# A planned attention-and-FFN kernel: transposes issued in groups, the planner's matmul price by stream and next load, plain heads on 128 rows, weights converted in pieces of 512 columns

## The chip, the core and the metric

The kernel runs on one core of a Trainium2 chip. The metric is device time in microseconds (us): a median over runs, and beside it one profiled execution, whose trace tells what each engine did. TensorE (PE) multiplies, VectorE (DVE), ScalarE (ACT) and GpSimd (POOL) do the elementwise work, and SyncE (SP) issues the DMAs.

## What is computed

Block-causal attention over 8 batches of 8 heads (576 tokens, 64 dimensions, blocks of 64), then a feed-forward network on all 4608 tokens:

```python
scores = scale * np.matmul(q, k.transpose(0, 1, 3, 2))
mask = block_i >= block_j
scores = np.where(mask, scores, -1000000000.0)
scores = scores - np.max(scores, axis=-1, keepdims=True)
attn = np.exp(scores)
attn = attn / (np.sum(attn, axis=-1, keepdims=True) + 1e-09)
x = np.matmul(attn, v)          # heads side by side: (4608, 512)
h = x @ w_in                    # 512 -> 2048
g = np.maximum(0.01 * h, h)
out = g @ w_out                 # 2048 -> 512
```

q, k and v are 32-bit floats; w_in and w_out arrive as 64-bit floats; the kernel takes their bits apart and makes 32-bit values of them.

## The kernel before

**Precision.** A product that must be exact to 32 bits is made of faster matmuls: each operand is split into a high part and a low remainder (`xh`, `xl`; `wih`, `wil`; `gh`, `gl`; `pth`, `ptl`), and three partial products are summed. Heads called plain use whole 32-bit operands instead; one such matmul is two records in the trace.

**Work.** Each of the 64 heads goes through scores into `p_s`, a mask, row maxima (`nm`), the exponentials with their sums (`prow`, `sums`), reciprocals (`rec`), normalising, transposes of `prow` through PE against the identity into the two banks of `p_t`, and the product with V, which is then copied into `xr`. A head's scores come in two parts: tiles 0 to 3 first (eight matmuls in a full head), then tile 4 (four matmuls of 288 columns), which uses the same PSUM and so waits for the exponentials of the first part. The eight heads of the first batch are done in two halves: "lo" (tokens 0 to 319) and "hi" (320 to 575), all with plain products, and with plain scores but for one "hi" head. Heads 8 to 63 are "full" and split.

**FFN.** Tokens go through the FFN in 18 chunks of 256. `split_x` makes `xh` and `xl`; then for each of eight units `u`, `ffn1` does two blocks of twelve matmuls into `p_h` (line 734), followed by the activation into `g`, its split into `gh` and `gl`, and `ffn2` does two blocks of six into `p_o` (line 753). A chunk can start when the heads of its tokens are done, so the first starts after the eight "lo" heads, the second after the "hi" heads, and the third only after eight full heads.

**Weights.** `weight_piece` loads 256 KB into one of six `raw` buffers, makes a 32-bit value in one of six `val` buffers by an ACT copy and two or three integer operations on DVE (lines 397, 401, 406; the sign of every third piece is done by ACT and POOL instead), and splits it. There are 64 pieces. Their converting runs beside the first sixteen heads. Full heads start when it is over, since some of their tiles take the space of the conversion.

**Order.** Nothing is issued in the order of the code. `Plan` collects every operation with its rank, costs and dependences, and a list scheduler at build time (`Plan.run`) walks through modelled time and, for each free engine, takes the ready operation of lowest rank. The constants RL to AHEAD set ranks relative to the head's number. Where PE has nothing ready early on, a `fill` matmul of the identity is inserted. The result is a fixed instruction order on each engine. In this order, transposes (kind "short") are woven one by one between the matmuls of an `ffn2` block (kind "long"):

```python
while a or b:
    if b:
        mixed.append(b.pop(0))
    if a:
        mixed.append(a.pop(0))
```

Of the kernel before, what the change touches and what calls it, by code (L numbers as in the profile page):

```python
# [17 lines left out]
P = 128  # L18
BLK = 64
D = 64  # L20
# [3 lines left out]
EPS = 1e-9  # L24
CH = 256

HS = 7
SIGNS = 3

WIDE = 256  # L30
RAWS = 6
VALS = 6

RL = 7.153
RP = 0.885
RB = 0.516
RT = 1.485
RV = 1.932
RX = -0.113
RN = -0.908  # L40

LEAD = 1.751
LAG = 1.627
RS = 0.514
RG = -0.26
OFF1 = 4.574
SL1 = 11.938
AHEAD = -0.663

LAT = 1550  # L50
HOLD = 567.499

PATIENCE = 424.599
FILL = 235
FILLTO = 12

# [1 line left out]
LOAD = 108  # L58
RATE = 0.4414
# [1 line left out]


class Plan:

# [34 lines left out]
    def run(self):  # L102
# [10 lines left out]
        free = dict.fromkeys(ready, 0)  # L113
        port = {"DVE": 0, "POOL": 0}
        order, now, moved, done = [], 0, 0, 0
        load, start, stream = -LOAD, 0, 0

        def offer(i):
            for k, choice in enumerate(self.ops[i][0]):
# [11 lines left out]
                if not left[j]:  # L131
                    offer(j)

        def multiply(matmuls):
            nonlocal load, start, stream
            for cost, fn in matmuls:
                if now < SLOW:
                    cost *= 2
                load = max(load + LOAD, start, now - 57)
                start = max(start + stream, load + 57, now)  # L140
                stream = cost
                order.append(fn)
            return start + stream

        def best(kind):
            found = [x for x in ready["PE"] if self.ops[x[1]][4] == kind and not ends[x[1]]]
            return min(found) if found else None

        for i in range(total):
            if not left[i]:  # L150
# [1 line left out]
        while done < total:  # L152
# [6 lines left out]
            for e, q in ready.items():  # L159
# [5 lines left out]
                if other:  # L165
                    open_ = port[other] <= now
                    can = [x for x in q if not ends[x[1]] and (open_ or (e == "DVE" and self.ops[x[1]][0][x[2]][0] == "DVE"))]
                    if not can:
                        wake.append(port[other])
                        continue  # L170
                    x = min(can)
                    q.remove(x)
                    heapq.heapify(q)
                elif e == "PE":
                    live = [x for x in q if not ends[x[1]]]
                    x = min(live)
                    short, long_ = best("short"), best("long")
                    if self.ops[x[1]][4] == "short" and not long_:
                        other_ = [y for y in live if self.ops[y[1]][4] != "short"]
                        if other_ and now < since[x[1]] + PATIENCE:  # L180
                            x = min(other_)
                    kind = self.ops[x[1]][4]
                    if kind == "long":
                        self.fill = None
                    if kind in ("short", "long") and short and long_:
                        a = [(c, f, short[1]) for c, f in self.ops[short[1]][0][0][1]]
                        b = [(c, f, long_[1]) for c, f in self.ops[long_[1]][0][0][1]]
                        mixed = []
                        while a or b:
                            if b:  # L190
                                mixed.append(b.pop(0))
                            if a:
                                mixed.append(a.pop(0))
                        at = {}
                        for c, f, i in mixed:
                            at[i] = multiply([(c, f)])
                        free[e] = start + stream
                        for y in (short, long_):
                            q.remove(y)
                            end(y[1], e, at[y[1]])  # L200
                        heapq.heapify(q)
                        continue
                    q.remove(x)
                    heapq.heapify(q)
                    free[e] = multiply(self.ops[x[1]][0][x[2]][1])
                    end(x[1], e, free[e])
                    continue
                else:
                    x = heapq.heappop(q)
# [48 lines left out]
def attention_ffn(ctx: ExitStack, tc: tile.TileContext, qk: bass.AP, v: bass.AP, w_in: bass.AP, w_out: bass.AP, out: bass.AP):  # L258
# [162 lines left out]
    def attention(i):  # L421
# [5 lines left out]

        qkt, qkey = qk_in[z], ("qkt", z)
        plain_s, plain_v = kind == "lo" or kind == "hi" and h < HS, kind != "full"
        rows = D if plain_s else P  # L430
        odd = kind == "lo" and z == 1
        sk = "h" if odd else "s"

# [3 lines left out]
        def row(t, n, c, w):  # L437
            at, c0 = {0: (3, 256), 1: (3, 0), 2: (4, 0)}[t] if odd else (t, 0)
            return prow[y][at][:n, c0 + c : c0 + c + w]
# [21 lines left out]
        rp = r0 - RP  # L461
        q_in, k_in = qkt[:rows, 0, qa:qe], qkt[:rows, 1, :ke]
        if plain_s:
            add(copying(qe - qa, lambda: q_in, lambda: q_in, by=scale), rp, [], [qkey])
            qkd = [qkey]
        else:
            qd, khd, kld = qs[z][:, qa:qe], kh[z][:, :ke], kl[z][:, :ke]
# [100 lines left out]
        for base, c0, w, items in tgroups[kind]:  # L568
            x = bank()

            def transpose(t, j, c, x=x):
                n = P if kind == "full" else qn[t]
                return RATE * n, lambda: nc.tensor.transpose(p_t[x][:, c : c + n], row(t, n, j * P, P), ident[:n, :n])  # L573

            add([("PE", [transpose(*y) for y in items])], r0 + RT, [k for t in sorted({a for a, _, _ in items}) for k in pkeys(t)], [("t", x)], kind="short")
            src = p_t[x][:, c0 : c0 + w]
            if plain_v:
                hi = ptf[:, base : base + w]
# [258 lines left out]
```

## Time and profile before

| | |
|---|---|
| median of 3 runs | 1193.65 us (1190.58 to 1194.34) |
| the profiled execution: its time, its span | 1194.37 us, 1192.3 us |
| busy share of the span | PE 99%, DVE 57%, ACT 55%, POOL 36% |
| chain that ended last | PE 96%, DVE 2%, ACT 1% |
| lines on that chain | p_o L753 33%, p_h L734 33%, p_t L573 9%, p_t L635 8% |
| granted clock, mean | 0.996 |
| read from memory, written | 64.57 MB, 9.44 MB |

The span is the time from the first to the last profiled instruction; the execution's own time is a little longer. A share of busy time is an average over stages, and matmuls overlap each other, so a PE that is always "busy" may still be late: what tells is the distance between the starts of matmuls.

### The profile page before, as it was taken

To read this page: it belongs to the slowest core of one execution; us is meant where nothing else is said; L and a number is where in the kernel's file an instruction comes from. 1 tells how busy PE (TensorE), PEld (TensorE's weight loads), DVE (VectorE), ACT (ScalarE), POOL (GpSimd) and SP (SyncE) were. 2 spreads that over 40 slices of the span, in tenths; PEclk is the share of its full clock that TensorE was granted. 3 is DMA by queue.
4 is the path that set the end of the run, shared out by engine and by line. 5 is a ranking of instruction groups with operands and counts; after the bars stand their busy time and mean duration, and the time that the engine had idled before them with its cause. 6 is when DMAs were issued, how large, how long until landed. Compare 5 with 4: busy or idle time off the path is not lost.

```text
span 1192.3 us, 21079 instructions
## 1 busy us (share of the span) xinstructions
PE 1175.5 (99%) x7778; PEld 1041.4 (87%) x7778; DVE 680.2 (57%) x1782; ACT 657.4 (55%) x1652; POOL 431.5 (36%) x505
## 2 busy tenths in 40 slices
PE   9999899899999999999999999999999999999998
PEld 7877789788899988898999988898998888899997
DVE  5999987766656666644444456665666666310000
ACT  6988866655655565554554455555555555422222
POOL 3233344324443443423332343443444343212222
PEclk9999999899999999999999999999999999999999
DMA  6656422211212111110211211112121210000000
GB/s 175 185 173 193 128 88 72 66 60 55 67 51 70 52 55 60 37 64 30 62 39 35 67 49 55 47 51 69 52 69 46 70 31 30 1 18 1 18 19 18
DMA packets 39592, 75.37 MB, mean 63 GB/s; under 512 B 4032, under 2 KB 23040, under 8 KB 39488
## 3 DMA queue, kind: packets, MB, share of 16 engines
q1 hardware_dynamic: 39488, 74.02, 20.2%
q8 instruction: 61, 1.00, 0.3%
q14 instruction: 43, 0.35, 0.1%
HBM read 64.57 MB, written 9.44 MB: 62 GB/s over the span
## 4 chain that ended last, share of the span: by engine, by line
PE 96%; DVE 2%; ACT 1%; DMA 0%; issue 0%; ACTq 0%; DVEq 0%
PE p_o L753 33%; PE p_h L734 33%; PE p_t L573 9%; PE p_t L635 8%; PE p_s L494 8%; PE p_t L625 2%; PE p_s L488 2%; PE p_o L806 2%; DVE nm L512 1%; PE p_h L488 0%; DVE ptl L284 0%; DVE prow L550 0%; DMA qk_in<-in_qk 0%; ACT prow L521 0%; DMA raw<-in_w_in 0%
## 5 line engine op out<-in xcount | busy, mean ns | idle before, releaser
L285 POOL TENSOR_TENSOR gl<-g,gh 128x512 fp32r<-128x512 f32 x136 | 176.8, 1300 | 460.6 <-ACT gh L274 311.3
L734 PE MATMUL p_h<-xh,wih 128*128 128x256 f32 x1152 | 323.2, 281 | 0.0
L734 PE MATMUL p_h<-xl,wih 128*128 128x256 f32 x1152 | 320.1, 278 | 1.1 <-DVE xl L284 1.1
L734 PE MATMUL p_h<-xh,wil 128*128 128x256 f32 x1152 | 319.9, 278 | 0.0
L521 ACT ACTIVATE prow<-p_s,nm 128x192 f32<-128x192 f32 (+4 forms) x308 | 161.8, 529 | 151.4 <-DVE nm L512 95.4
L573 PE MATMUL p_t<-ident,prow 128*128 128x128 f32 x960 | 239.7, 274 | 3.1 <-DVE ptl L284 0.9
L734 PEld LDWEIGHTS p_h<-xl,wih 128*128 128x128 f32 x1152 | 216.9, 188 | 4.6 <-DVE xl L284 1.3
L734 PEld LDWEIGHTS p_h<-xh,wih 128*128 128x128 f32 x1152 | 216.9, 188 | 4.5 <-issue 1.0
L753 PE MATMUL p_o<-wol,gh 128*128 128x512 f32 x576 | 219.9, 453 | 0.0
L734 PEld LDWEIGHTS p_h<-xh,wil 128*128 128x128 f32 x1152 | 217.0, 188 | 0.0
L741 ACT ACTIVATE g<-p_h 128x512 f32<-128x512 f32 x144 | 85.7, 595 | 234.4 <-PE p_h L734 234.1
L753 PE MATMUL p_o<-woh,gh 128*128 128x512 f32 x576 | 204.0, 426 | 0.0
L753 PE MATMUL p_o<-woh,gl 128*128 128x512 f32 x576 | 192.2, 415 | 0.0
L549 POOL TENSOR_SCALAR prow<-prow,rec 128x192 f32<-128x192 f32 (+4 forms) x214 | 119.1, 568 | 167.1 <-DVE rec L536 124.3
L284 DVE TENSOR_TENSOR ptl<-p_t,pth 128x512 fp32r<-128x512 f32 (+1 forms) x224 | 125.1, 567 | 63.0 <-ACT pth L274 59.6
L614 DVE TENSOR_TENSOR xr<-p_t,xr 64x64 f32<-64x64 f32 x112 | 50.4, 450 | 164.6 <-ACT xr L274 164.3
L573 PEld LDWEIGHTS p_t<-ident,prow 128*128 128x128 f32 x960 | 130.2, 141 | 13.9 <-DVE ptl L284 1.9
L512 DVE TENSOR_REDUCE nm<-p_s 128x1 f32<-128x192 f32 (+4 forms) x308 | 139.7, 486 | 4.6
L753 PEld LDWEIGHTS p_o<-wol,gh 128*128 128x128 f32 x576 | 108.6, 188 | 35.6
L753 PEld LDWEIGHTS p_o<-woh,gh 128*128 128x128 f32 x576 | 105.5, 189 | 28.1 <-issue 2.6
L274 ACT CAST pth<-p_t 128x384 fp32r<-128x384 f32 (+3 forms) x175 | 81.5, 469 | 63.9 <-PE p_t L573 59.5
L753 PEld LDWEIGHTS p_o<-woh,gl 128*128 128x128 f32 x576 | 96.6, 189 | 20.0
(77 smaller groups left out, 1623.9 us busy)
## 6 DMA issues: line engine op xcount, KB each, us to landing
qk_in<-in_qk SPq DMA_DIRECT2D x56, 576.0 KB, 3.7
v_stage<-in_v SPq DMA_DIRECT2D x56, 160.0 KB, 2.2
out<-ob SPq DMA_DIRECT2D x35, 256.0 KB, 2.0
raw<-in_w_in SPq DMA_DIRECT2D x32, 256.0 KB, 3.0
raw<-in_w_out SPq DMA_DIRECT2D x32, 256.0 KB, 3.2
qk_in<-in_qk SPq DMA_DIRECT2D x8, 160.0 KB, 3.0
vf<-in_v SPq DMA_DIRECT2D x8, 160.0 KB, 3.2
vf<-in_v SPq DMA_DIRECT2D x8, 128.0 KB, 2.6
```

The source lines that it names most:

```text
L274: one = lambda: nc.scalar.copy(dst(), src())
L284: ("DVE+" if sb else "DVE", dve(n), lambda: nc.vector.tensor_sub(dst(), one(), two())),
L285: ("POOL", pool2(n), lambda: nc.gpsimd.tensor_sub(dst(), one(), two())),
L494: go = lambda ap=ap, cols=cols, kk=kk, k0=k0, k1=k1, first=first, last=last: nc.tensor.matmul(ap, qs[z][:, cols], kk[:, k0:k1], start=firs ...
L512: [("DVE", dve(kw[t]), lambda t=t, ap=ap, flat=flat: nc.vector.tensor_reduce(nm[z][: qn[t], t : t + 1], ap[: qn[t]], axis=AX.X if flat els ...
L521: nc.scalar.activation(o, ap[: qn[t]], AF.Exp, bias=nm[z][: qn[t], t : t + 1], scale=1.0, accum_out=sums[z][: qn[t], t : t + 1])
L549: ("POOL", pool1(kw[t]), lambda: nc.gpsimd.tensor_scalar(p(), p(), by, 1.0, op0=ALU.mult, op1=ALU.mult)),
L573: return RATE * n, lambda: nc.tensor.transpose(p_t[x][:, c : c + n], row(t, n, j * P, P), ident[:n, :n])
L635: nc.tensor.matmul(to, vs[z][:, j, :], src, start=start, stop=stop)
L734: nc.tensor.matmul(hh[:, i, :], w[:, d, f * P : (f + 1) * P], x[:, d, :], start=k == 0, stop=k == len(terms) - 1)
L741: add([("ACT", act(512), lambda: nc.scalar.activation(g, hh, AF.Prelu, alpha=0.01))], rank, [("h", z)], ["g"])
L753: nc.tensor.matmul(p_o[m], a[:, i, m * P : (m + 1) * P], w[:, 2 * u + i, :], start=u == 0 and k == 0, stop=u == NU - 1 and k == 5,)
```

## The change

It has four parts. The planner no longer weaves transposes into `ffn2` blocks: each group of transposes is one operation, issued in one piece. Its price of a matmul becomes the larger of two things, the stream of the one ahead and a load (108 ns) that begins when the one ahead has started, and not before the operation's inputs are there; a transpose is priced at a stream of 27 ns. All "hi" heads have plain scores (HS 8), and plain heads take 128 rows of q and k, where the array holds q and k twice, with half the scale. Weights are converted in 32 pieces of 512 columns (512 KB) with rings of three, and every fifth piece has its sign done by ACT and POOL. All ranks and the delay for an operation's second choice of engine (HOLD) have new numbers.

```diff
-HS = 7
-SIGNS = 3
-WIDE = 256
-RAWS = 6
-VALS = 6
+HS = 8
+SIGNS = 5
+WIDE = 512
+RAWS = 3
+VALS = 3
...
-RS = 0.514
+RS = 1.479
...
-HOLD = 567.499
-
-PATIENCE = 424.599
+HOLD = 247.855
...
-        def multiply(matmuls):
-            nonlocal load, start, stream
+        def multiply(matmuls, at):
+            nonlocal start, stream
             for cost, fn in matmuls:
                 if now < SLOW:
                     cost *= 2
-                load = max(load + LOAD, start, now - 57)
-                start = max(start + stream, load + 57, now)
+                start = max(start + stream, max(start, at) + LOAD, now)
                 stream = cost
                 order.append(fn)
             return start + stream
...
-                    if kind in ("short", "long") and short and long_:
...
-                    free[e] = multiply(self.ops[x[1]][0][x[2]][1])
+                    x = heapq.heappop(q)
+                    if self.ops[x[1]][4] == "long":
+                        self.fill = None
+                    free[e] = multiply(self.ops[x[1]][0][x[2]][1], since[x[1]])
...
-        rows = D if plain_s else P
+        rows = P
...
-            add(copying(qe - qa, lambda: q_in, lambda: q_in, by=scale), rp, [], [qkey])
+            add(copying(qe - qa, lambda: q_in, lambda: q_in, by=scale / 2), rp, [], [qkey])
...
-                return RATE * n, lambda: nc.tensor.transpose(p_t[x][:, c : c + n], row(t, n, j * P, P), ident[:n, :n])
+                return 27, lambda: nc.tensor.transpose(p_t[x][:, c : c + n], row(t, n, j * P, P), ident[:n, :n])
```

**Around the first p_h.** On PE, from the last part of the "lo" stage to the first FFN matmul, before (`p_o<-ident` is a fill, `p_t<-ident,prow` a transpose, `p_s<-qk_in` a plain score):

```order
L806 MATMUL p_o_110<-ident 128x128 x8
L488 MATMUL p_s<-qk_in_87 128x448
L806 MATMUL p_o_110<-ident 128x128 x17
L573 MATMUL p_t_107<-ident,prow_3_76 128x128
L573 MATMUL p_t_107<-ident,prow_4_77 128x128
...
L806 MATMUL p_o_110<-ident 128x128 x6
L488 MATMUL p_s<-qk_in_87 128x288 x2
L734 MATMUL p_h_108<-xh,wih 128x256
```

and now:

```order
L771 MATMUL p_o_110<-ident 128x128 x8
L453 MATMUL p_s<-qk_in_87 128x448
L771 MATMUL p_o_110<-ident 128x128 x2
L538 MATMUL p_t_107<-ident,prow_3_76 128x128
L538 MATMUL p_t_107<-ident,prow_4_77 128x128
...
L771 MATMUL p_o_110<-ident 128x128 x4
L699 MATMUL p_h_108<-xh,wih 128x256
```

Seventeen fills fewer stand between the last product of a "lo" head and the first p_h, and the two scores of 288 columns have gone behind it. On DVE, the operations ahead of `xl`, which that p_h needs, before:

```order
L284 TENSOR_TENSOR wil<-val_131,wih 128x2x128
L397 TENSOR_SCALAR val_132<-val_132 128x256
L397 TENSOR_SCALAR val_133<-val_133 128x256
L284 TENSOR_TENSOR wol<-val_129,woh 128x256
L401 SCALAR_TENSOR_TENSOR val_132<-raw_126,val_132 128x256
L401 SCALAR_TENSOR_TENSOR val_133<-raw_127,val_133 128x256
L397 TENSOR_SCALAR val_134<-val_134 128x256
L406 SCALAR_TENSOR_TENSOR val_133<-raw_127,val_133 128x256
L401 SCALAR_TENSOR_TENSOR val_134<-raw_128,val_134 128x256
L284 TENSOR_TENSOR xl<-xr_104,xh 128x1024
```

and now:

```order
L500 TENSOR_SCALAR rec_100<-sums_98 128x1
L501 RECIPROCAL rec_100<-rec_100 128x1
L366 SCALAR_TENSOR_TENSOR val_126<-raw_123,val_126 128x512
L515 TENSOR_SCALAR prow_4_77<-prow_4_77,rec_100 128x576
L371 SCALAR_TENSOR_TENSOR val_126<-raw_123,val_126 128x512
L249 TENSOR_TENSOR xl<-xr_104,xh 128x1024
```

`xl` has moved ahead of most of the weight operations; it stands behind two of 512 columns and one normalising.

**Full heads that have one FFN unit each.** On PE before, between the products of the sixth and the seventh full head, from the end of a second score part to the next head's scores:

```order
L494 MATMUL p_s<-kl_93,qs_89 128x288
L573 MATMUL p_t_107<-ident,prow_4_77 128x128
L573 MATMUL p_t_107<-ident,prow_2_75 128x128
...
L573 MATMUL p_t_106<-ident,prow_0_73 128x128
L494 MATMUL p_s<-kh_90,qs_88 128x448
L494 MATMUL p_s<-kh_90,qs_88 128x64
L494 MATMUL p_s<-kl_92,qs_88 128x448
```

and now, between the products of the fifth and the sixth, from the end of a group of eight transposes:

```order
L538 MATMUL p_t_107<-ident,prow_3_1354 128x128
L538 MATMUL p_t_107<-ident,prow_4_1355 128x128
L718 MATMUL p_o_111<-woh,gh_114 128x512 x2
L718 MATMUL p_o_111<-wol,gh_114 128x512 x2
L718 MATMUL p_o_111<-woh,gl_116 128x512 x2
L699 MATMUL p_h_108<-xh,wih 128x256
L699 MATMUL p_h_108<-xl,wih 128x256
L699 MATMUL p_h_108<-xh,wil 128x256
```

Before, nothing of the FFN was left there to put between transposes and scores; now a block of each kind stands in every head of this stage.

**Full heads that have two units each.** On ACT, between the first and the last exponential of a first score part, before:

```order
L521 ACTIVATE prow_3_1612,sums_99<-p_s,nm_97 128x448
L521 ACTIVATE prow_0_1609,sums_99<-p_s,nm_97 64x64
L741 ACTIVATE g<-p_h_108 128x512
L521 ACTIVATE prow_1_1610,sums_99<-p_s,nm_97 128x192
L274 CAST gh_113<-g 128x512
L521 ACTIVATE prow_2_1611,sums_99<-p_s,nm_97 128x320
```

and now:

```order
L486 ACTIVATE prow_3_76,sums_98<-p_s,nm_96 128x448
L486 ACTIVATE prow_0_73,sums_98<-p_s,nm_96 64x64
L239 CAST gh_113<-g 128x512
L486 ACTIVATE prow_1_74,sums_98<-p_s,nm_96 128x192
L486 ACTIVATE prow_2_75,sums_98<-p_s,nm_96 128x320
```

The activation `g` no longer stands among the exponentials.

## Rows read from the trace of the kernel before

**Rows 1.** Windows: per engine busy us (instructions), then granted clock, DMA share, GB/s.

```profile
60.00:140.00 80.00, 78.14 (x454) 60.80 (x454) 73.00 (x213) 67.92 (x177) 26.99 (x32) 1.00 0.58 177
140.00:253.00 113.00, 104.56 (x674) 93.14 (x672) 87.56 (x229) 75.08 (x199) 46.29 (x60) 0.95 0.23 74
253.00:1192.00 939.00, 935.48 (x6312) 841.09 (x6310) 473.81 (x1174) 465.79 (x1126) 338.86 (x378) 1.00 0.15 45
```

**Rows 2.** Timeline of a full head: start us, us, engine, line, operation, out<-in, count.

```profile
315.35 0.45 PE L635 MATMUL p_t<-pth,vs 128*128 128x512 f32 x2
...
316.97 0.40 PE L494 MATMUL p_s<-kh,qs 128*128 128x448 f32 x2
...
318.09 0.31 PE L734 MATMUL p_h<-xh,wih 128*128 128x256 f32 x1
...
318.89 0.20 DVE L663 TENSOR_TENSOR xr<-p_t,xr 64x64 f32<-64x64 f32 x1
...
319.67 0.23 DVE L663 TENSOR_TENSOR xr<-p_t,xr 64x64 f32<-64x64 f32 x1
...
320.85 0.39 PE L753 MATMUL p_o<-woh,gh 128*128 128x512 f32 x1
...
321.52 0.59 ACT L741 ACTIVATE g<-p_h 128x512 f32<-128x512 f32 x1
...
322.68 0.40 PE L753 MATMUL p_o<-woh,gh 128*128 128x512 f32 x1
...
323.62 0.20 ACT L521 ACTIVATION_READ_ACCUMULATOR prow<-p_s,nm 128x1 f32 x1
...
324.52 0.29 PE L494 MATMUL p_s<-kh,qs 128*128 128x288 f32 x1
...
325.05 0.39 PE L753 MATMUL p_o<-woh,gh 128*128 128x512 f32 x1
```

**Rows 3.** Timeline of PE after the last head.

```profile
1100.42 0.62 PE L753 MATMUL p_o<-woh,gh 128*128 128x512 f32 x2
...
1103.17 0.28 PE L734 MATMUL p_h<-xh,wih 128*128 128x256 f32 x1
```

**Rows 4.** Timeline around the first p_h.

```profile
49.54 2.05 PE L806 MATMUL p_o<-ident 128*128 128x128 f32 x16
...
52.01 1.04 ACT L274 CAST xh<-xr 128x1024 fp32r<-128x1024 f32 x1
...
56.36 1.15 PE L573 MATMUL p_t<-ident,prow 128*128 128x128 f32 x9
...
57.35 1.50 PE L806 MATMUL p_o<-ident 128*128 128x128 f32 x12
...
57.50 1.21 DVE L284 TENSOR_TENSOR xl<-xr,xh 128x1024 fp32r<-128x1024 f32 x1
...
58.78 1.23 PE L488 MATMUL p_s<-qk_in 64*128 64x288 f32 x4
...
59.94 0.38 PE L734 MATMUL p_h<-xh,wih 128*128 128x256 f32 x1
```

**Rows 5.** The page, DMA issues: count, KB each, median us from issue to landing.

```profile
qk_in<-in_qk SPq DMA_DIRECT2D x56, 576.0 KB, 3.7
raw<-in_w_in SPq DMA_DIRECT2D x32, 256.0 KB, 3.0
```

**Rows 6.** Groups by line and form, DVE: count | busy us, mean ns | idle before.

```profile
L401 DVE SCALAR_TENSOR_TENSOR val<-raw,val 128x256 int32<-128x256 int32 x64 | 27.0, 434 | 0.0
```

**Rows 7.** Timeline of PE, three places between 140 and 253 us; in brackets idle before.

```profile
140.22 0.38 PE L734 MATMUL p_h<-xh,wih 128*128 128x256 f32 x1
...
226.38 0.80 PE L494 MATMUL p_s<-kh,qs 128*128 128x448 f32 x2 [1.67 <-ACT prow L521]
...
252.94 0.28 PE L734 MATMUL p_h<-xh,wih 128*128 128x256 f32 x1
```

**Rows 8.** Window in the same stretch, columns as in rows 1.

```profile
225.80:232.60 6.80, 6.21 (x21) 5.66 (x22) 4.53 (x15) 1.94 (x6) 0.99 (x2) 0.50 0.26 89
```

More of the change, by code (lines that the diff above doesn't have):

```diff
@@ L25 @@
 CH = 256
-HS = 7
-SIGNS = 3
-WIDE = 256
-RAWS = 6
-VALS = 6
[L34 to L43, printed above, removed]
-RS = 0.514
[L45 to L48, printed above, removed]
+HS = 8
[3 more added lines that the diff above has]
+VALS = 3
+RL = 4.863
+RP = 0.785
+RB = 0.315
+RT = 1.294
+RV = 1.99
+RX = -1.905
+RN = -1.001
+LEAD = 1.99
+LAG = 2.037
+RS = 1.479
+RG = -0.264
+OFF1 = 4.287
+SL1 = 12.111
+AHEAD = -0.615
 LAT = 1550
-HOLD = 567.499
-PATIENCE = 424.599
+HOLD = 247.855
 FILL = 235
@@ L115, in run @@
         order, now, moved, done = [], 0, 0, 0
-        load, start, stream = -LOAD, 0, 0
+        start, stream = 0, 0
         def offer(i):
@@ L143, in multiply @@
             return start + stream
-        def best(kind):
-            found = [x for x in ready["PE"] if self.ops[x[1]][4] == kind and not ends[x[1]]]
-            return min(found) if found else None
         for i in range(total):
@@ L174, in run @@
                 elif e == "PE":
[L175 to L183, printed above, removed]
-                        self.fill = None
-                    if kind in ("short", "long") and short and long_:
[L186 to L204, printed above, removed]
-                    free[e] = multiply(self.ops[x[1]][0][x[2]][1])
+                    x = heapq.heappop(q)
+                    if self.ops[x[1]][4] == "long":
+                        self.fill = None
+                    free[e] = multiply(self.ops[x[1]][0][x[2]][1], since[x[1]])
                     end(x[1], e, free[e])
@@ L572, in transpose @@
                 n = P if kind == "full" else qn[t]
-                return RATE * n, lambda: nc.tensor.transpose(p_t[x][:, c : c + n], row(t, n, j * P, P), ident[:n, :n])
-            add([("PE", [transpose(*y) for y in items])], r0 + RT, [k for t in sorted({a for a, _, _ in items}) for k in pkeys(t)], [("t", x)], kind="short")
+                return 27, lambda: nc.tensor.transpose(p_t[x][:, c : c + n], row(t, n, j * P, P), ident[:n, :n])
+            add([("PE", [transpose(*y) for y in items])], r0 + RT, [k for t in sorted({a for a, _, _ in items}) for k in pkeys(t)], [("t", x)])
             src = p_t[x][:, c0 : c0 + w]
```

## Prediction

> **What bounds the kernel now.** I read the windows first. From 253 us to the end PE is busy 935.5 of 939 us at full clock, while DVE is idle half the time; only a few us can be lost there. From 60 to 140 us, where weights are converted beside the "hi" heads, PE is busy 78 of 80 us, but DVE 73 and ACT 68 as well. From 140 to 253 us PE has 104.6 of 113 us and a mean granted clock of 0.95 [rows 1]. Then the timelines: PE's "busy" counts the fills ahead of the first p_h, and a slow matmul as much as a fast one. So time can be had in two places: before the first p_h, and between 140 and 253 us.
>
> To weigh instruction orders I need PE's time for each kind of work, from start to start. Twenty-four p_h take 320.85 − 318.09 = 2.76 us, 0.115 each; the product with V of a full head 1.62, its first score part 1.12, its second 0.53 [rows 2]. Twelve p_o alone take 2.75 us, 0.229 each [rows 3]. Nine transposes in a group take 57.35 − 56.36 = 0.99 us, 0.110 each; the six fills behind them 1.43 us, 0.238 each; two plain scores of 288 columns 1.16 us [rows 4].
>
> **Grouping the transposes.** Six p_o with four transposes woven in take 322.68 − 320.85 = 1.83 us [rows 2]; six alone would be 1.375. A woven transpose thus costs 0.114 us, a grouped one 0.110 [rows 2, 3, 4]. The order before has 767 woven ones. I take no gain, with 767 × 0.004 = 3 us as the other bound: weaving hid nothing.
>
> The Trainium skill would see it otherwise: "TensorE: Matmul & The Clock Gate", section "Step-by-step: what each phase is for", says that PE pulls a weight load ahead into a background buffer, so that it runs under the matmul before. By its formula for back-to-back matmuls a woven transpose would then cost an estimated 56 ns, and grouping would add some 41 us. This trace does not agree, with 0.114 us.
>
> **The first p_h.** Between the last product of a "lo" head (49.54 us) and the first p_h (59.94) lie 10.40 us [rows 4]. The order before has 31 fills there, one plain score of 448 columns, nine transposes and the two of 288 columns: 31 × 0.238 + 0.90 (1.16 × 448/576) + 0.99 + 1.16 = 10.4, so the prices hold. What PE waits for is `xl`: ACT had finished `xh` at 53.05, but DVE came to `xl` at 57.50 only, behind weight operations [rows 4]. Now 14 fills stand there, the 448 columns and the transposes: 3.3 + 0.90 + 0.99 = 5.2 us. That agrees with 53.05 + 1.21 for `xl`, about 54.3 us, as the earliest p_h, 4.8 us behind the product. I take −5.2 us; the bounds are 0 (the weight operations of 512 columns hold `xl` up as much as those of 256 did) and −5.6.
>
> The very first load doubles, since plain heads take 128 rows: 160 KB more. By 3.0 us for 256 KB and 3.7 for 576 KB [rows 5] that is 0.7 × 160/320 = +0.35 us; the later loads lie beside other work. Matmul prices go by columns, which stay; I take nothing for the 128 rows.
>
> **The "hi" stage.** It loses nothing I can name and is full of PE work. Moved into it are the two scores of 288 columns, +1.16; moved out behind its last product is one second score part, −0.53. The eighth head's plain scores cost 0.90 + 1.16 = 2.06 instead of 0.53 × 1024/576 = 0.94, so +1.1. Sum +1.7 us. The conversion has half the operations at twice the width; one costs between one and two of the old ones, so the 27.0 us of line 401 (434 ns each [rows 6]) become 14 to 28. PE's work hides this, so I count nothing; if DVE were late it would show as PE waiting for `wih` (third rival).
>
> **140 to 253 us.** From the p_h behind the last "hi" product (140.22) to the one behind the ninth full head's product (252.94) pass 112.7 us [rows 7]. The order before has there 228 p_h, 108 p_o, 135 transposes, nine products and nine heads' scores: 26.2 + 24.7 + 14.9 + 14.6 + 14.9 = 95.3 us. So 17.4 us are lost. The reason is in the order: PE has used up the FFN units of the first two chunks, and the transposes and scores of one head and the next stand side by side, each waiting for softmax; at 226.38 PE stood 1.67 us for an exponential [rows 7]. Around these waits the granted clock fell to 0.50, the level of 1.2 GHz, for 6.8 us [rows 8], which alone costs 3.4.
>
> Now every full head of this stage has one block of p_o and one of p_h between its eight transposes and the next seven, and another of each further on. The work is 240 p_h and one score part more: 27.6 + 24.7 + 14.9 + 14.6 + 15.4 = 97.2 us. Between a first score part and the second stand 8 × 0.110 + 6 × 0.229 + 12 × 0.115 + 7 × 0.110 = 4.4 us. The softmax between them took 323.82 − 318.09 = 5.73 us in a steady head [rows 2], but with 1.0 us of other operations in it that the order now has elsewhere (two additions on DVE, 0.20 and 0.23; `g` on ACT, 0.59); without them it is 4.7. So some waits remain. I take the clock's 3.4 us as regained and half of the other 14 as lost still: 7 us, bounds 0 and 17.4. The stage then takes 104.2 us, −8.5. The twelve p_h done here are missing later: −1.4.
>
> **The steady heads.** Before, 2.76 + 2 × 1.83 = 6.4 us stand between the score parts, and the second began 0.70 us after the exponentials were read out [rows 2]. Now twelve p_o, eight transposes and twelve p_h stand there, 2.75 + 0.88 + 1.38 = 5.0 us, in 43 heads. `g` and the two additions have left the chain: 5.73 − 0.59 − 0.43 = 4.7 us. That fits by 0.3 us, so I count +2 us for a head now and then; the bounds are 0 and the second rival.
>
> **Sum**, against this execution's span: 1192.3 − 5.2 + 0.35 + 1.7 − 8.5 − 1.4 + 2 = 1181.3 us. The execution took 2.07 us more than its span and 0.72 more than the median of the runs: 1181.3 + 1.35 = **1182.6 us**.
>
> **Rivals.**
> - *The waits come back elsewhere.* The stage to 253 us loses its 17.4 us as before (in-order engines behind heavier operations) and `xl` gains only half: 1182.6 + 10.4 + 2.6 = 1195.6 us. For it: DVE is 91% busy in the stage before [rows 1]. Against it: the FFN blocks that were missing now stand there.
> - *The shorter cover of the steady heads*, slower. If the chain keeps the length of before, 5.73 us against 5.0 of cover, each of 43 heads waits 0.7 us: about 1211. At 0.35 us a head the gain is gone. Against it: `g` is out of the order there.
> - *The rings of three hold up the weights*, slower. A buffer's turn is a landing plus the operations that read it. A landing of 512 KB lies 0.6 us above one of 256 [rows 5], and each of some three readers may take up to one old duration longer, 0.43 us [rows 6]: 1.9 us a turn, 32/3 turns, 20 us until the last weight. Full heads wait for that one; of which I let two thirds reach PE: 1182.6 + 14 = 1197.
> - *Loads were hidden by weaving*: 767 × 0.055 = 42 us if a woven transpose cost half of a grouped one, so about 1225. This is what the rule of the Trainium skill named above ("TensorE: Matmul & The Clock Gate", "Step-by-step: what each phase is for") would do here. The pair of 0.114 and 0.110 us speaks against it.
>
> **The numbers.** Forecast 0.64, with its own range 1169 (nothing lost to 253 us, 3 us for the grouping) to 1190; waits elsewhere 0.17; steady heads 0.10; rings 0.07; hidden loads 0.02. The range to hold 8 in 10 is 1169 to 1198 us. About 0.3% (3.6 us) is what a measurement can tell from no change. Faster, below 1190: 0.62 (nearly all of the forecast). The same, up to 1197: 0.22 (most of the first rival, parts of the next two and of the forecast). Slower: 0.16.
>
> **What would show it.** First p_h near 55 us; the ninth full head's product done near 241 us; no granted clock of 0.50 between 150 and 250 us; grouped transposes 0.110 us apart; the second score part of steady heads without a wait for `prow`. Wrong it would be if PE waits there in every head, if p_h waits for `wih` or `xl`, or if the last weight comes after 140 us.

## The result, and the profile after

The changed kernel takes 1174.64 us (median of 4 runs, 1172.86 to 1178.77) against 1192.99 us (median of 4 runs, 1190.58 to 1194.34) of the kernel before: ratio 0.9853, 95% interval 0.9822 to 0.9885. The forecast was 1182.6 us with a range of 1169 to 1198; the direction and the range held, and the time lies 8.0 us below the forecast.

The page after begins with the busy times and, further down, the slices of the granted clock and the DMA issues (KB each, median us to landing):

```profile
PE 1159.5 (99%) x7742; PEld 1053.2 (90%) x7742; DVE 676.7 (58%) x1756; ACT 611.4 (52%) x1535; POOL 432.3 (37%) x438
...
PEclk9999999999999999999999999999999999999999
...
raw<-in_w_in SPq DMA_DIRECT2D x16, 512.0 KB, 4.9
```

The busy shares of PE, DVE and POOL are those of before within a point, so they tell nothing. No slice of the clock is under 9 tenths. A weight load of 512 KB now takes 4.9 us where 256 KB took 3.0 [rows 5].

The windows of the changed kernel, cut at the same places of the program as [rows 1] and [rows 7] (first the "hi" stage from 60 us on, then from the last "hi" product to the ninth full head's, then the rest):

```profile
60.00:131.90 71.90, 69.21 (x405) 55.54 (x403) 67.71 (x135) 56.86 (x120) 23.05 (x17) 1.00 0.62 193
131.90:233.40 101.50, 99.81 (x686) 91.51 (x687) 87.89 (x233) 79.56 (x216) 37.55 (x44) 1.00 0.28 87
233.40:1172.00 938.60, 934.79 (x6300) 860.56 (x6299) 473.33 (x1256) 427.86 (x1074) 355.73 (x348) 1.00 0.15 45
```

In the middle window PE's idle time is 1.7 us, where it was 8.4 us of 113 before, and the granted clock is 1.00 instead of 0.95. The last window is as long as before.

PE's starts at the places of [rows 4] and [rows 7], the timeline of all engines round the first p_h, then of PE at the two ends of the stage:

```profile
47.10 2.05 PE L771 MATMUL p_o<-ident 128*128 128x128 f32 x16
...
48.51 1.03 ACT L239 CAST xh<-xr 128x1024 fp32r<-128x1024 f32 x1
...
49.93 0.69 DVE L371 SCALAR_TENSOR_TENSOR val<-raw,val 128x512 int32<-128x512 int32 x1
...
50.53 1.22 DVE L249 TENSOR_TENSOR xl<-xr,xh 128x1024 fp32r<-128x1024 f32 x1
...
51.98 0.37 PE L699 MATMUL p_h<-xh,wih 128*128 128x256 f32 x1
```

```profile
131.89 0.40 PE L459 MATMUL p_s<-kh,qs 128*128 128x288 f32 x1 [0.57 <-ACT prow L486]
...
233.35 0.42 PE L459 MATMUL p_s<-kh,qs 128*128 128x448 f32 x2
```

`xl` still stands behind a weight operation on DVE, but is done at 51.75 us, and p_h starts 0.2 us later.

I keep one ledger for every kernel, with the same cuts: the last "lo" product, the first p_h, the last "hi" product, the ninth full head's product, the end. "Lost" in the fourth stage is its length less its matmuls at the prediction's prices (95.2 us of work before, 97.2 after).

| us | to last "lo" product | to first p_h | "hi" stage | to ninth full head | lost there | rest |
|---|---|---|---|---|---|---|
| before | 49.5 | 10.4 | 80.3 | 112.7 | 17.5 | 939.3 |
| changed | 47.1 | 4.9 | 79.9 | 101.5 | 4.3 | 938.6 |

So of 20.3 us of span, 11.3 came from the stage between the products, 5.5 from the wait for the first p_h, 2.4 from ahead of it, and 1.1 from the other two.

A steady head, timeline of all engines, for comparison with [rows 2]:

```profile
503.29 0.28 PE L699 MATMUL p_h<-xh,wih 128*128 128x256 f32 x1
...
504.70 0.40 PE L459 MATMUL p_s<-kh,qs 128*128 128x448 f32 x2
...
505.81 0.65 PE L718 MATMUL p_o<-woh,gh 128*128 128x512 f32 x2
...
508.61 1.03 PE L538 MATMUL p_t<-ident,prow 128*128 128x128 f32 x8
...
510.33 0.20 ACT L486 ACTIVATION_READ_ACCUMULATOR prow<-p_s,nm 128x1 f32 x1
...
510.86 0.29 PE L459 MATMUL p_s<-kh,qs 128*128 128x288 f32 x1
```

The exponentials are read out 0.33 us before the second score part comes up, and PE waits for nothing. All that PE waits for in the whole kernel (line waited for, us in total, times, longest) is this:

```profile
PE p_t L538 <- ACT prow L516: 2.2, 2, 1.6
PE p_s L459 <- ACT prow L486: 1.7, 3, 1.0
PE p_o L771 <- POOL ident masks.py:199: 1.4, 1, 1.4
PE p_s L453 <- ACT prow L486: 1.2, 1, 1.2
PE p_s L453 <- ACT qk_in L242: 1.1, 1, 1.1
PE p_h L699 <- DVE wil L249: 0.8, 1, 0.8
```

None of these is behind 238 us.

### The profile page after: what moved, and what is told of

Its sections match the earlier page's. It is cut to its first block, busy times and chain, and to the rows that moved or that the text cites. A ratio compares the mean times of both kernels' runs of the same rounds, so it can differ in the third digit from the quotient of the medians.

```text
span 1172.0 us, 21030 instructions
## 1 busy us (share of the span) xinstructions
PE 1159.5 (99%) x7742; PEld 1053.2 (90%) x7742; DVE 676.7 (58%) x1756; ACT 611.4 (52%) x1535; POOL 432.3 (37%) x438
## 4 chain that ended last, share of the span: by engine, by line
PE 85%; DVE 6%; ACT 5%; issue 1%; DMA 1%; SPq 0%; POOL 0%; ACTq 0%; DVEq 0%
PE p_h L699 31%; PE p_o L718 31%; PE p_t L538 8%; PE p_t L600 7%; PE p_s L459 7%; ACT prow L486 2%; DVE nm L477 1%; DMA raw<-in_w_in 1%; PE p_t L590 1%; DVE val L366 1%; DVE val L371 1%; ACT prow L516 1%; DVE rec L500 1%; PE p_s L453 1%; ACT xr L239 0%
## 5 line engine op out<-in xcount | busy, mean ns | idle before, releaser
L718 PE MATMUL p_o<-woh,gh 128*128 128x512 f32 x576 | 186.4, 405 | 0.0
L718 PE MATMUL p_o<-wol,gh 128*128 128x512 f32 x576 | 179.3, 392 | 0.0
L718 PE MATMUL p_o<-woh,gl 128*128 128x512 f32 x576 | 179.1, 392 | 0.0
L706 ACT ACTIVATE g<-p_h 128x512 f32<-128x512 f32 x144 | 86.1, 598 | 139.8 <-PE p_h L699 137.7
L514 POOL TENSOR_SCALAR prow<-prow,rec 128x448 f32<-128x448 f32 (+3 forms) x151 | 96.8, 649 | 141.5 <-DVE rec L501 115.2
L538 PE MATMUL p_t<-ident,prow 128*128 128x128 f32 x960 | 130.2, 274 | 2.2 <-ACT prow L516 2.2
L239 ACT CAST gh<-g 128x512 fp32r<-128x512 f32 x136 | 83.8, 617 | 91.8 <-PE p_o L718 91.7
L249 DVE TENSOR_TENSOR ptl<-p_t,pth 128x512 fp32r<-128x512 f32 (+1 forms) x224 | 117.3, 561 | 23.5 <-ACT pth L239 23.1
L718 PEld LDWEIGHTS p_o<-woh,gl 128*128 128x128 f32 x576 | 108.2, 188 | 24.4
L538 PEld LDWEIGHTS p_t<-ident,prow 128*128 128x128 f32 x960 | 109.8, 141 | 13.5 <-issue 2.5
L718 PEld LDWEIGHTS p_o<-woh,gh 128*128 128x128 f32 x576 | 97.1, 189 | 12.5 <-issue 1.1
```

What stands on the lines that cost most here:

```text
L239: one = lambda: nc.scalar.copy(dst(), src())
L249: ("DVE+" if sb else "DVE", dve(n), lambda: nc.vector.tensor_sub(dst(), one(), two())),
L514: ("POOL", pool1(kw[t]), lambda: nc.gpsimd.tensor_scalar(p(), p(), by, 1.0, op0=ALU.mult, op1=ALU.mult)),
L538: return 27, lambda: nc.tensor.transpose(p_t[x][:, c : c + n], row(t, n, j * P, P), ident[:n, :n])
L706: add([("ACT", act(512), lambda: nc.scalar.activation(g, hh, AF.Prelu, alpha=0.01))], rank, [("h", z)], ["g"])
L718: nc.tensor.matmul(p_o[m], a[:, i, m * P : (m + 1) * P], w[:, 2 * u + i, :], start=u == 0 and k == 0, stop=u == NU - 1 and k == 5,)
```

## The experiments

All were timed against the kernel before, which had medians of 1193.0 to 1194.2 us in them.

**The parts one at a time.** My theory was that grouping works through the order: woven transposes drag a block of p_o with them whatever its rank, and so use up the FFN units of the first two chunks before the last heads of the stage need them. The rivals: it is the ranks, or the wide conversion. First grouping and the price rule alone, with all constants, rows and pieces of before:

```diff
-                load = max(load + LOAD, start, now - 57)
-                start = max(start + stream, load + 57, now)
+                start = max(start + stream, max(start, at) + LOAD, now)
...
-                    if kind in ("short", "long") and short and long_:
```

> The kernel before with the planner's part alone: transposes in groups, the price by stream and next load. The order has 26 fills ahead of the first p_h (31 before), and p_o units left over for the full heads of the stage to 253 us (13 done at the sixth, 15 before). Theory of the spread FFN (my prediction's step for 140 to 253 us: weaving had used up the p_o units there, grouped transposes leave them): the stage loses 5 to 9 us less, the first p_h comes 1 to 3 us earlier; about 1183 us, ratio 0.990 to 0.994. Rival, the wide weights give it all: no change, 0.998 to 1.002. Rival, weaving hid the loads: 1.02 to 1.035.

1185.9 us, ratio 0.993 (0.9913 to 0.9946). The time is as expected. The stage fell from 112.7 to 101.6 us and lost 6.4, so 11.1 less than before, more than the 5 to 9 expected. But the first p_h came later, at 62.3 us, not earlier: the last "lo" product was done only at 54.3. That part of my expectation was wrong.

Then the wide conversion alone, in the order with weaving:

```diff
-SIGNS = 3
-WIDE = 256
-RAWS = 6
-VALS = 6
+SIGNS = 5
+WIDE = 512
+RAWS = 3
+VALS = 3
```

> The kernel before with the weights' part alone: pieces of 512 columns, rings of three, every fifth sign by ACT and POOL. Theory of the spread FFN: the stage to 253 us still loses its 15 to 18 us, since the units are used up as before (15 p_o units at the sixth full head, as before); the first p_h may come 1 to 3 us earlier, since half the operations stand ahead of xl; ratio 0.996 to 1.000. Rival, the conversion's fewer operations are the gain: 0.985 to 0.992. Rival of my prediction, the rings of three hold up the weights: 1.004 to 1.012, with the last weight operation past 145 us.

1196.85 us, 1.0035 (1.0023 to 1.0047): a little slower, which my theory's range missed. The last weight came at 146.9 us instead of 143.5, past the 145 of the rival with the rings, and the ratio lies just under that rival's 1.004. The stage lost 22.7 us.

The 128 rows and the eighth plain head alone:

```diff
-HS = 7
+HS = 8
...
-        rows = D if plain_s else P
+        rows = P
...
-            add(copying(qe - qa, lambda: q_in, lambda: q_in, by=scale), rp, [], [qkey])
+            add(copying(qe - qa, lambda: q_in, lambda: q_in, by=scale / 2), rp, [], [qkey])
```

> The kernel before with plain heads on 128 rows, all eight hi heads plain. My prediction: the longer first load +0.35 us, the eighth head's scores +1.1 us, matmuls of 128 rows as long as those of 64; the order is new everywhere, which I can't price: ratio 0.998 to 1.004. Rival, 128 rows are slower to stream: the distance of two plain scores of 288 columns rises above 1.16 us.

1194.33 us, 0.9999 (0.9987 to 1.0011). No difference in the total. The rival is out: two plain scores of 288 columns took 1.06 to 1.17 us, where they took 1.16 before, and one of 448 columns 0.40 to 0.75, where it took 0.95. So "as long as those of 64" was wrong too, to the other side. Nothing of it reached the total: the "hi" stage with its eighth plain head took 83.2 us, 2.9 more than before, and the stage behind it 116.2, 3.5 more.

All rank constants and HOLD alone, with weaving:

```diff
-RL = 7.153
...
+RL = 4.863
...
-HOLD = 567.499
+HOLD = 247.855
```

> The kernel before with the new ranks and HOLD alone, transposes still woven. The order has 25 fills ahead of the first p_h (31 before), but all 16 p_o units of the first two chunks are used up at the sixth full head already (15 before). Theory of the spread FFN: the first p_h comes 2 to 5 us earlier, and the stage to 253 us loses as much as before or more, 17 to 22 us; ratio 0.996 to 1.002. Rival, the ranks give the gain: 0.985 to 0.992.

1205.43 us, 1.0108 (1.0093 to 1.0122): slower, against what I expected. The "hi" stage took 84.3 us, 4.0 more than before, and the stage behind it lost 22.2; after the sixth full head the p_h and the p_o of all 16 units of the first two chunks were done. Behind the waits that follow, the granted clock falls to 0.50 for 6.8 us, as in [rows 8]; the window, with the columns of [rows 1]:

```profile
233.60:240.40 6.80, 5.84 (x22) 5.13 (x23) 4.78 (x13) 3.24 (x9) 3.25 (x4) 0.50 0.26 89
```

The four parts alone add up to +0.7%, together they give −1.5%. So none has a price of its own.

**Weaving put back** into the changed kernel, all else as changed:

```diff
-                    x = heapq.heappop(q)
+                    x = min(y for y in q if not ends[y[1]])
...
+                    if x in (short, long_) and short and long_:
...
+                        while a or b:
+                            if b:
+                                mixed.append(b.pop(0))
+                            if a:
+                                mixed.append(a.pop(0))
```

> The changed kernel with the weaving put back: whenever transposes and a block of p_o are both ready, they are issued alternately, whatever the block's rank (769 woven transposes); all constants and the price by stream and next load stay. Theory: grouping is worth something only through the order, since weaving pulls a block of p_o forward with each group of transposes and uses up the first two chunks' FFN units early (after the sixth full head 16 and 15.5 units are issued instead of 15 and 12). The stage from the last hi product to the ninth full head's product then loses 15 to 20 us instead of 4.3, the first p_h stays near 52 us, and the time is 1184 to 1190 us, ratio to the kernel before 0.992 to 0.998. Rival, the loss was in the price rule and the ranks, not in weaving: 1172 to 1178 us, ratio 0.983 to 0.987. Rival, loads are hidden by weaving: 769 times 0.055 us less, about 1135 us.

1191.89 us, 0.9985 (0.9967 to 1.0002): nearly the whole gain is gone, a little more than expected, and all units were used up as the theory said. But the stage lost 13.9 us instead of 4.3, less than the 15 to 20 expected: the last "hi" product came 5.7 us later, which I had not expected, and the rest took 943.6 us, 5.0 more, with twelve more p_h in it (1.4 us). PE's longest waits between the two products:

```profile
PE p_t L564 <- DVE ptl L275: 2.8, 2, 2.0
PE p_t L564 <- DVE xr L654: 1.5, 2, 0.8
PE p_s L485 <- ACT prow L512: 1.1, 2, 0.9
PE p_t L564 <- DVE p_s L496: 1.1, 2, 0.7
```

Here transposes wait for the operations of one `p_t` bank or the other, and the granted clock fell to one half twice, for 3.4 us each; the first:

```profile
227.80:231.20 3.40, 3.16 (x12) 2.68 (x13) 2.50 (x8) 2.46 (x11) 0.88 (x2) 0.50 0.02 5
```

**Weaving only in the later heads**, where nothing runs short: the same edit with another condition.

```diff
-                    if x in (short, long_) and short and long_:
+                    if x in (short, long_) and short and long_ and x[0] > 28:
```

> The same weaving, but only for heads whose rank is over 28, so that the order up to the ninth full head is that of the changed kernel and 651 transposes of the later heads are woven. Theory: weaving and grouping cost PE the same where nothing runs short, so 1172 to 1179 us, ratio 0.983 to 0.988, a woven transpose 0.112 to 0.116 us and no waits in the later heads. Rival, loads are hidden by weaving: 651 times 0.055 us less, about 1138 us, ratio 0.955. Rival, grouping itself saves time in the later heads: slower by over 5 us, ratio above 0.989.

1176.02 us, 0.9839 (0.9813 to 0.9866), the same as the changed kernel. One woven block, from its first p_o to the first of the next; six p_o and four transposes start in between:

```profile
508.86 0.39 PE L744 MATMUL p_o<-woh,gh 128*128 128x512 f32 x1
...
510.71 0.40 PE L744 MATMUL p_o<-woh,gh 128*128 128x512 f32 x1
```

1.85 us, less six p_o at 0.229, leaves 0.119 for a woven transpose in this block; the grouped ones cost 0.109 (508.61 to 510.86 above, less twelve p_h at 0.115, over eight). The rest of the kernel took 940.9 us, 2.3 more for 651 woven transposes. Grouping as such is worth at most that; weaving hid no loads. Summed over the trace from each start to the next, p_o and transposes of the rest took 433.4 us woven and 427.0 grouped, but the same 3036 p_h took 350.7 us beside woven transposes and 355.8 beside grouped ones. So most of what grouping takes off the transposes comes back on the p_h.

**Grouping, price and ranks**, without the wide pieces and the rows:

```diff
-HS = 8
-SIGNS = 5
-
-WIDE = 512
-RAWS = 3
-VALS = 3
+HS = 7
+SIGNS = 3
+
+WIDE = 256
+RAWS = 6
+VALS = 6
...
-        rows = P
+        rows = D if plain_s else P
...
-            add(copying(qe - qa, lambda: q_in, lambda: q_in, by=scale / 2), rp, [], [qkey])
+            add(copying(qe - qa, lambda: q_in, lambda: q_in, by=scale), rp, [], [qkey])
```

> Grouping, the price by stream and next load, and all the rank constants and HOLD of the changed kernel; the pieces of 256 columns, the rings of six and three and the 64 rows of plain heads stay as before. Theory: the ranks, which alone made the kernel slower by 1.1%, pay only once no weaving pulls p_o forward; then the two together are nearly the whole change: first p_h near 54 us (15 fills ahead of it), loss in the stage to the ninth full head 4 to 8 us, 1174 to 1180 us, ratio 0.984 to 0.989. Rival, the ranks pay only with the pieces of 512 columns: no better than grouping and price alone, 1183 to 1188 us, ratio 0.991 to 0.995.

1189.46 us, 0.9959 (0.9935 to 0.9982): a miss, and worse even than the rival's 1183 to 1188. The first p_h was earlier (55.9 us), but in the conversion stage PE stood still once; its timeline, with DVE and POOL:

```profile
127.37 0.28 PE L699 MATMUL p_h<-xh,wil 128*128 128x256 f32 x1
...
132.12 0.79 PE L459 MATMUL p_s<-kh,qs 128*128 128x448 f32 x2 [4.46 <-ACT prow L486]
```

```profile
128.45 1.56 POOL L250 TENSOR_TENSOR kl<-qk_in,kh 128x576 fp32r<-128x576 f32 x1 [3.80 <-ACT kh L239]
128.65 1.63 DVE L366 SCALAR_TENSOR_TENSOR val<-raw,val 128x256 int32<-128x256 int32 x1
...
130.29 0.11 DVE L470 MEMSET p_s<- 64x64 f32 x1
...
130.44 0.76 DVE L477 TENSOR_REDUCE nm<-p_s 128x1 f32<-128x576 f32 x1
```

The scores were there, but the mask and the maxima stood on DVE behind weight operations until 130.29 us, one of which took 1.63 us beside POOL's `kl`. During the wait, at 130.7 us, the granted clock fell to 0.50 for 6.8 us. The stage took 84.3 us, 4 more than before.

**One part taken back from the whole.** The pieces of 256 columns:

```diff
-SIGNS = 5
-
-WIDE = 512
-RAWS = 3
-VALS = 3
+SIGNS = 3
+
+WIDE = 256
+RAWS = 6
+VALS = 6
```

> The changed kernel with the conversion of before: pieces of 256 columns, rings of six, six and three. Theory: the wide pieces are worth what they bring before the first p_h: 21 fills instead of 14 stand there, 7 times 0.238 or 1.7 us, and the last weight comes later by up to 8 us, at little cost to PE; 1174 to 1179 us, ratio 0.985 to 0.989, first p_h at 53 to 56 us. Rival, the wide pieces carry the conversion stage: xl and wil come late again, first p_h near 60 us and the hi stage longer by 2 to 4 us, 1181 to 1186 us, ratio 0.990 to 0.995.

1179.08 us, 0.9873 (0.9846 to 0.99): as expected; its interval does not tell it from the whole change. First p_h at 57.8 us, later than expected; the "hi" stage took 75.5 us, 4.4 less than in the changed kernel, and the stage behind it lost 9.7.

The 64 rows and seven plain heads:

```diff
-HS = 8
+HS = 7
...
-        rows = P
+        rows = D if plain_s else P
...
-            add(copying(qe - qa, lambda: q_in, lambda: q_in, by=scale / 2), rp, [], [qkey])
+            add(copying(qe - qa, lambda: q_in, lambda: q_in, by=scale), rp, [], [qkey])
```

> The changed kernel with plain heads on 64 rows again and seven plain hi heads; ranks, price, grouping and wide pieces stay. Theory: the 128 rows cost and bring nothing by themselves, and the eighth plain head only shifts work; 23 fills instead of 14 but no transposes stand ahead of the first p_h, which comes at about 53 us; 1173 to 1180 us, ratio 0.983 to 0.989. Rival, the eighth plain head takes a split of q and k off DVE and ACT in the conversion stage and that stage depends on it: waits there as in the kernel with ranks and price alone, 1181 to 1188 us, ratio 0.990 to 0.996.

1181.34 us, 0.9887 (0.9862 to 0.9913): between theory and rival. First p_h at 54.9 us, the stage lost 9.3 us, with three waits for `xr` and one of 1.4 us for `wih`, and the plain scores took 0.95 and 1.16 us again, as before. So the part that did nothing alone may be worth some 0.3% here; the intervals overlap, and I don't call it shown.

The wide pieces, grouping and price with the ranks, HOLD and rows of before:

```diff
-HS = 8
+HS = 7
...
-RL = 4.863
...
+RL = 7.153
...
-HOLD = 247.855
+HOLD = 567.499
...
-        rows = P
+        rows = D if plain_s else P
...
-            add(copying(qe - qa, lambda: q_in, lambda: q_in, by=scale / 2), rp, [], [qkey])
+            add(copying(qe - qa, lambda: q_in, lambda: q_in, by=scale), rp, [], [qkey])
```

> Grouping, price and the pieces of 512 columns with rings of three; the ranks, HOLD and the 64 rows stay as before. Theory: the wide pieces help only together with the ranks that were chosen with them (alone they cost 0.3%), so this is near grouping and price alone: 1182 to 1189 us, ratio 0.991 to 0.997. Rival, the wide pieces are what relieves the conversion stage whatever the ranks: ratio 0.984 to 0.989, 1174 to 1180 us.

1188.72 us, 0.9951 (0.9933 to 0.9968), as the theory said. The stage lost 14.5 us.

One rank of before, LAG:

```diff
-LAG = 2.037
+LAG = 1.627
```

> The changed kernel with one rank constant of before, LAG 1.627 instead of 2.037: the p_o blocks come earlier, so that after the sixth full head of the stage 15 and 14 units of the first two chunks are used instead of 15 and 12, and after the eighth 16 and 16 instead of 16 and 15. Theory, the units left over for the last heads of the stage decide: the stage loses 6 to 10 us instead of 4.3 and the time is 1176 to 1181 us, ratio 0.986 to 0.990. Rival, one block more or less per head does not matter once transposes are grouped: 1172 to 1176 us, ratio 0.983 to 0.986.

1174.51 us, 0.9831 (0.9802 to 0.986). The total is the rival's. The stage went the theory's way and past its 6 to 10 us: it lost 11.7, the granted clock was 0.50 for 6.8 us, and the waits came back where the units had run out:

```profile
224.80 0.80 PE L459 MATMUL p_s<-kh,qs 128*128 128x448 f32 x2 [1.63 <-ACT prow L486]
...
231.59 0.66 PE L538 MATMUL p_t<-ident,prow 128*128 128x128 f32 x4 [1.39 <-DVE xr L579]
```

But the "hi" stage was 5.2 us shorter, and the rest took 934.7 us with 1.4 us more work in it. In the order of its steady heads most p_h stand in one block of 24, and both groups of transposes between the score parts. Whether that pace was the order's or one execution's was open, so the last run took each half of it.

**LAG by stage:** the changed kernel's order up to the ninth full head, then that of the run above:

```diff
-                ffn2(c, u, rank + (nxt - i) * LAG / num + 0.003)
+                ffn2(c, u, rank + (nxt - i) * (LAG if i <= 2 * H else 1.627) / num + 0.003)
```

> LAG as in the changed kernel for the FFN units ranked beside the second batch's first eight full heads, 1.627 for all later ones. The order up to the ninth full head is that of the changed kernel, the steady heads have the order of the run with LAG of before (both groups of transposes and both blocks of p_o between the score parts, then 24 p_h). Theory, the steady heads of that order are faster by 0.11 us each, as the trace of that run shows: the stage loses about 4 us as in the changed kernel and the rest takes about 935 us instead of 938.6: 1168 to 1172 us, ratio 0.979 to 0.982. Rival, the pace of the steady heads belonged to that one execution and not to the order: 1173 to 1177 us, ratio 0.983 to 0.986.

**1168.83 us, 0.9803 (0.9789 to 0.9816), faster than both kernels.** The same windows:

```profile
131.40:232.90 101.50, 99.82 (x686) 91.62 (x687) 87.91 (x233) 79.58 (x216) 37.50 (x44) 1.00 0.27 87
232.90:1166.40 933.50, 929.73 (x6300) 856.45 (x6299) 458.59 (x1234) 469.76 (x1155) 296.46 (x289) 1.00 0.14 45
```

As the theory said; the interval lies below that of the changed kernel. The stage is that of the changed kernel to a tenth, the rest 5.1 us shorter with the same number of matmuls. So the pace is the order's. PE waits for nothing behind 238 us in either.

The ledger of all runs; "units" tells, of the 16 FFN units of the first two chunks, how many have their p_h and how many their p_o issued ahead of the last product of the eighth full head:

| kernel | ratio | first p_h, us | lost to ninth head, us | units | last weight, us |
|---|---|---|---|---|---|
| before | 1 | 59.9 | 17.5 | 16, 16 | 143.5 |
| rows alone | 0.9999 | 57.4 | 18.5 | 16, 16 | 144.2 |
| wide alone | 1.0035 | 58.7 | 22.7 | 16, 16 | 146.9 |
| ranks alone | 1.0108 | 57.9 | 22.2 | 16, 16 | 150.3 |
| weaving back | 0.9985 | 52.2 | 13.9 | 16, 16 | 138.8 |
| grouping, price, wide | 0.9951 | 56.7 | 14.5 | 16, 16 | 139.8 |
| grouping, price, ranks | 0.9959 | 55.9 | 8.3 | 16, 16 | 149.5 |
| narrow pieces | 0.9873 | 57.8 | 9.7 | 16, 16 | 142.1 |
| 64 rows | 0.9887 | 54.9 | 9.3 | 16, 16 | 140.2 |
| LAG of before | 0.9831 | 54.0 | 11.7 | 16, 16 | 138.8 |
| grouping and price | 0.993 | 62.3 | 6.4 | 16, 15 | 146.9 |
| weaving late | 0.9839 | 52.0 | 4.3 | 16, 15 | 136.2 |
| changed | 0.9853 | 52.0 | 4.3 | 16, 15 | 135.5 |
| LAG by stage | 0.9803 | 51.5 | 4.3 | 16, 15 | 135.0 |

The four kernels that have one unit's p_o left for the ninth head lose 4.3 to 6.4 us, the ten with none 8.3 to 22.7. Three of the four share one order up to there, and the ten differ in more than the units, so the table alone does not show the cause. LAG comes nearest: one rank changed, the units gone, 11.7 us lost; the rank of the changed kernel back in this stage alone, 4.3.

## Why the prediction was right, and where it was off

**Grouping neutral: right in the total.** 2.3 us over 651 transposes is within the bound of 3. But the prices were not the near equals of the prediction, 0.109 us grouped against 0.119 woven; the total is small because the p_h got dearer by 5.1 us, a term the prediction did not have. That part was luck. The rival of hidden loads is ruled out. The rule of the Trainium skill that stood behind it ("TensorE: Matmul & The Clock Gate", "Step-by-step: what each phase is for": a weight load is pulled ahead and runs under the matmul before) would have made the kernel with late weaving an estimated 36 us faster; its rest was 2.3 us longer.

**The first p_h: −4.85 predicted, −8.0 measured.** The step itself was right, −5.2 against −5.5 (10.4 to 4.9 us). What failed is the term beside it: I had charged the doubled first load with +0.35 us and nothing else to the "lo" stage, and the last "lo" product came 2.4 us earlier. The kernels with wide pieces have it at 46.5 to 49.0 us, those with narrow ones at 48.7 to 54.3. The rows may have a part in it: of the kernels with wide pieces the three with 64 rows have it at 48.5 to 48.6 us, four of the five with 128 rows at 46.5 to 47.2. Which operation makes the difference is not separated.

**"hi" stage: +1.7 predicted, −0.4 measured.** The step that failed is "I take nothing for the 128 rows". PE's starts around a plain score of 448 columns, before and in the changed kernel:

```profile
66.13 0.28 PE L734 MATMUL p_h<-xh,wil 128*128 128x256 f32 x1
66.33 1.02 PE L488 MATMUL p_s<-qk_in 64*128 64x448 f32 x2
...
67.50 0.28 PE L734 MATMUL p_h<-xl,wih 128*128 128x256 f32 x1
```

```profile
59.11 0.28 PE L699 MATMUL p_h<-xh,wil 128*128 128x256 f32 x1
59.23 0.91 PE L453 MATMUL p_s<-qk_in 128*128 128x448 f32 x2
...
60.09 0.28 PE L699 MATMUL p_h<-xl,wih 128*128 128x256 f32 x1
```

From the p_h ahead of it to the second p_h behind it pass 1.37 us before and 0.98 now. Two scores of 288 columns between a p_h and a product with V cost 0.19 us less in the same way (1.64 and 1.45). Six of the one kind and seven pairs of the other stand in this stage now, an estimated 3.7 us off. By the prediction's prices the work grew by 1.8 us, by these it shrank by an estimated 1.9. "It loses nothing I can name" was wrong as well, and the loss did not shrink: PE's idle time here was 1.9 us before and is 2.7 in the changed kernel (80.00 less 78.14 [rows 1] and 71.90 less 69.21), with waits of 1.2 us for `prow` and 0.8 for `wil`. The price and ranks without the wide pieces show what such waits can be: DVE's weight operations held up a head's mask and maxima, and one wait lasted 4.46 us.

**140 to 253 us: −8.5 predicted, −11.3 measured.** The mechanism was right: FFN blocks left over for the waits of the last heads, no granted clock of 0.50 there. The term that was mis-sized is "half of the other 14 as lost still", 7 us; 4.3 were lost. The ninth product was done at 233.4 us, not 241, since each stage before was shorter too. One reading of the order was too wide: not every head of the stage has a block of p_h, since all 16 units have theirs at the seventh product, and the eighth head has p_o alone. What I had not said is why the units last: the ranks of the changed kernel alone, with weaving, made it worse, and without weaving they kept a unit back only together with both the wide pieces and the 128 rows.

**Later: +0.6 predicted (−1.4 and +2), −0.7 measured.** No steady head waits. The chain from the end of the first score part to the exponentials read out, 505.81 to 510.53, is 4.72 us where I had 4.7, and the cover, 505.81 to 510.86, is 5.05 where I had 5.0; the +2 us was not needed.

Of the rivals, "the waits come back elsewhere" is what the kernels with 16 and 16 units do. The shorter cover of the steady heads cost nothing. The rings of three held nothing up in the changed kernel, where the last weight came 8 us earlier, though a landing of 512 KB of w_in took 1.9 us longer than one of 256 (4.9 and 3.0) and not the 0.6 of that rival's sum; beside the old order it came 3.4 us later with them and the wide pieces together. The terms are −3.1, −2.1, −2.8 and −1.3 us from the sum, all to the same side.

What stays open: how much of the total the 128 rows are worth, and why p_h cost less in the order with blocks of 24, with no wait in either.

## What to carry to other kernels

Where a scheduler pulls work forward as a pair, look at what that work was to cover later: here weaving cost little at the place where it stood, and its price was paid heads later, when the last ones before the next supply had nothing left to put between their waits. Parts of a tuned schedule have no prices of their own, four that add up to +0.7% apart gave −1.5% together, so test a part by taking it out of the whole as well as alone. Read the prices of a changed operand again from the trace: the scores on 128 rows were priced as before and cost less. Cut the span at fixed places of the program and keep a ledger of length less priced work: it showed that one rank was right in one stage and wrong in another, where the total showed no difference.

## What the runs showed of the hardware

One and the same number of matmuls, without waits at a full granted clock, took 938.6 us in one order and 933.5 in another. Summed from each start to the next, the 3036 p_h of the rest took 355.8 us in the changed kernel and 349.8 in the one with LAG by stage, the p_o 357.6 and 355.3, the second score parts 24.5 and 27.6, and all else the same within 0.2. In most steady heads of the changed kernel twelve p_h stand between transposes and the second score part and twelve between that and the next transposes, 1.46 and 1.42 us:

```profile
509.40 0.37 PE L699 MATMUL p_h<-xh,wih 128*128 128x256 f32 x1
...
510.86 0.29 PE L459 MATMUL p_s<-kh,qs 128*128 128x288 f32 x1
...
511.38 0.28 PE L699 MATMUL p_h<-xh,wih 128*128 128x256 f32 x1
...
512.80 0.93 PE L538 MATMUL p_t<-ident,prow 128*128 128x128 f32 x7
```

In the kernel with LAG by stage the 24 stand together in most heads, 2.74 us:

```profile
314.55 0.28 PE L699 MATMUL p_h<-xh,wih 128*128 128x256 f32 x1
...
317.29 0.62 PE L718 MATMUL p_o<-woh,gh 128*128 128x512 f32 x2
```

There the score part behind the transposes is dearer instead. What makes these differences no row shows.

A plain score of 448 columns on 128 rows cost 0.39 us less than on 64, among matmuls of 128 rows (1.37 and 0.98 us above). An operation of DVE that took 0.43 us in the mean before [rows 6] took 1.63 us while POOL's `kl` ran (128.45 to 130.01 us in the run with grouping, price and ranks); not every one is slowed so, one at 84.03 us of that run took 0.43 beside POOL. Twice as wide, the integer operations of the conversion cost less than twice: 128x512 on line 366 had a mean of 0.754 us, against 0.434 for 128x256 [rows 6], or medians of 0.676 and 0.414, and the group fell from 27.0 to 23.9 us.
